# One-token attention and gated MLP over a 65,536-row cache: VectorE looped over heads 1 to 7, q projected in wide rows, the output projection in row form

## Chip, cores and metric

One NeuronCore of a Trainium2 chip. The metric is device time of one launch in microseconds (us). A profiled span is about 1.6 us shorter than the time of its launch (666.87 and 665.2 us before). A ratio is the mean time of one kernel's runs over the mean of the other's of the same rounds, so it is not quite the ratio of the medians that are quoted. A gain is clear of noise where the interval of the ratio leaves out 1. In the profiles PE is TensorE (matrix products) and PEld its weight loads, DVE is VectorE, ACT ScalarE, POOL GpSimd; SyncE issues the loads.

## The reference

```python
# bf16; x [1,1,512]; k_cache, v_cache [1,8,65536,128]; wq [512,4096]; wo [4096,512]
# w_gate, w_up [512,1792]; w_down [1792,512]
n = layernorm(x)
q = (n @ wq) as 32 heads of 128            # 4 query heads share one k/v head
s = q . k * 128**-0.5;  p = softmax(s);  o = p . v
h = x + o.reshape(1,1,4096) @ wo
m = layernorm(h)
out = h + (sigmoid(m @ w_gate) * (m @ w_up)) @ w_down
```

K and V are 268 MB of the 282 MB that are read. Every byte is used once for one token.

## The kernel before

SyncE issues loads into a ring of four 4 MB slots. A block is 4 MB, 16,384 rows of one head; K0 to K31 and V0 to V31 number the blocks over all eight heads. A K block is transposed by VectorE in eight pieces, TensorE makes scores of it; after four blocks comes the softmax; V blocks of the head before go through TensorE in between. Every load waits for its slot:

```python
order = [("wq", 0)]
order += [("K", b) for b in range(NR)]                   # NR = 4 blocks per head, NB = 32
for b in range(NR, NB):
    order += [("K", b), ("V", b - NR)]
order += [("V", NB-4), ("V", NB-3), ("V", NB-2), ("V", NB-1), ("wg", 0), ("wu", 0), ("wd", 0)]
# slot i % 4; a K slot is freed by VectorE's memset F{b} behind its eight transposes,
# a V slot by the last matmul PV{b} on it. wo is loaded into ktw (the transposed K) behind
# V(NB-4), and waits for the last score, S{NB-1}.
```

The program is a list of operations for each engine, written out one by one, except that TensorE's list of heads 1 to 7 is a loop (rounds must be equal, semaphores are counted down at the end of a round):

```python
def run(e, eng):                       # SyncE, GpSimd, ScalarE, VectorE: all written out
    seen = {}
    for o in self.ops[e]:
        put(e, eng, o, waits_of(o, seen, 0, False))
def run_pe(eng):                       # TensorE (head and tail cut)
    ...
    with eng.Fori(0, rounds):
        for o, w in zip(pe[c[0]:c[1]], plans[0]):
            put("pe", eng, o, w)
        for k, n in self.loop_sems.items():
            eng.sem_inc(..., -n)
```

The q projection and the output projection for 28 of the 32 heads:

```python
for kt in range(4):
    for n in range(NQ):                                  # 128 matmuls of 128 columns
        e.matmul(ps(1, 0, 128, 0, 32), lhsT=xz[:, kt*63 + 31-n : kt*63 + 63-n],
                 rhs=wq_v[:, kt, n*128:(n+1)*128], ...)
def project(rows, src, deps, last=False):                # 4 matmuls of one column for each row r
    for r in rows:
        for nt in range(4):
            e.matmul(ps(YT, nt, nt+1), lhsT=<wo row r, every 4th column from nt>, rhs=src[:, r:r+1], ...)
```

Compiled, VectorE's stream has 30,720 bytes, TensorE's 111,296, ScalarE's 9,280. The Trainium skill ("Perfetto Trace Analysis", The 4-stage abstract model) gives 64 bytes an instruction: 480, 1,739 and 145 instructions.

## Time and profile before

| | before |
|---|---|
| time, median of 4 runs | 666.88 us (666.58 to 667.7) |
| profiled span | 665.2 us |
| TensorE / VectorE / ScalarE busy | 63% / 53% / 6% |
| load queue, share of 16 engines' span | 99.0% |
| last V part: its first 3 MB reach TensorE | 646.46 us |
| up weights reach TensorE | 657.53 us |

From the page of the kernel before: span and busy rows. In part 2 each digit is the busy share of one fortieth of the span, in tenths; "DMA" is the mean of the sixteen DMA engines. Part 3 lists the DMA queues: q1 is the load queue, the two "instruction" queues are sequencers (an engine's instruction feeders) that fetch their own programs. A line has packets, MB, and the share of the sixteen engines' span.

```profile
span 665.2 us, 5117 instructions
PE 419.9 (63%) x2545; PEld 84.9 (13%) x1777; DVE 350.8 (53%) x441; ACT 39.7 (6%) x119; POOL 5.4 (1%) x12
...
DMA  9999999999999999999999999999999999999995
...
q1 hardware_dynamic: 11560, 282.33, 99.0%
q8 instruction: 6, 0.10, 0.1%
q14 instruction: 5, 0.04, 0.0%
```

The chain that ended last, as shares of the span:

```profile
DMA 72%; DVE 21%; PE 6%; issue 1%; SPq 0%; ACT 0%
```

The loads are the bound. VectorE's share of the chain is transposes that began because a K block had just landed. The interesting question is what, with DMA busy all the time, can still change. The landings at the end show where it is decided. Here is TensorE's timeline at the end (start, duration, what; in brackets its idle time just before, and what ended it):

```profile
629.43 3.61 PE L500 MATMUL PS<-ring,PT_sb 128*16 128x512 bf16 x32 [8.11 <-DMA ring<-in_A_v_cache_dram]
639.14 3.61 PE L500 MATMUL PS<-ring,PT_sb 128*16 128x512 bf16 x32 [6.10 <-DMA ring<-in_A_v_cache_dram]
646.46 3.61 PE L500 MATMUL PS<-ring,PT_sb 128*16 128x512 bf16 x32 [3.70 <-DMA ring<-in_A_v_cache_dram]
657.53 1.66 PE L581 MATMUL PS<-ring,hc 128*1 128x448 bf16 x16 [1.33 <-DMA ring<-in_B_w_up_dram]
```

These are V29, V30, the first 3 MB of V31, and the up weights. TensorE waits for each of them.

**How the lag of an engine is read.** A load is split over sixteen DMA engines, and each posts one completion increment. The Trainium skill ("DMA: Bandwidth & Descriptors", Why a DMA increments its semaphore by 16 and not by 1) says that only the full 16 means that all data has landed; in this trace too each load leaves 16 increments (4-byte packets on the load queue), and the reader starts behind the last. The last one's time minus the median of the sixteen is called *lag* below; *spread* is the last minus the first. No view of the profile shows it; a script computed it from the starts of these packets. The matmuls that wait begin about 0.5 us behind them (V30: last packet 638.63, matmul 639.14 us). The DMA packet records of the kernel before give:

| load | K1 | K8 | K16 | K24 | K31 | V30 |
|---|---|---|---|---|---|---|
| lag, us | 1.38 | 1.57 | 1.99 | 3.00 | 3.07 | 3.78 |

The median engine takes 9.71 us per load throughout. Single engines fall behind, in steps, and the steps coincide with packets of the instruction queues: 16 KB at 22, 77, 113, 615, 623 and 657 us, 8 KB at 56, 221, 224, 426 and 613 us. The 32 KB load packet behind an 8 KB fetch takes 1.59 or 1.88 us, where 1.22 us is the median. Behind a 16 KB fetch (TensorE's, 0.93 to 1.13 us) it takes 1.71 to 1.76 us. So one block of TensorE's costs about 1.5 us, one of VectorE's 1.0 us (0.33 for the fetch, 0.66 for the longer packet). At K24 four of the sixteen increments stand clearly apart from the rest, 1.32, 1.43, 1.62 and 3.00 us behind the median: this fits one TensorE block on each of three engines, and three VectorE blocks on a fourth. On this reading a TensorE block makes the worst lag up to K8, and VectorE's blocks from K16 on.

### The profile page before, as it was taken

To read this page: it belongs to the slowest core of one execution; us is meant where nothing else is said; L and a number is where in the kernel's file an instruction comes from. 1 tells how busy PE (TensorE), PEld (TensorE's weight loads), DVE (VectorE), ACT (ScalarE), POOL (GpSimd) and SP (SyncE) were. 2 spreads that over 40 slices of the span, in tenths; PEclk is the share of its full clock that TensorE was granted. 3 is DMA by queue.
4 is the path that set the end of the run, shared out by engine and by line. 5 is a ranking of instruction groups with operands and counts; after the bars stand their busy time and mean duration, and the time that the engine had idled before them with its cause. 6 is when DMAs were issued, how large, how long until landed. Compare 5 with 4: busy or idle time off the path is not lost.

```text
span 665.2 us, 5117 instructions
## 1 busy us (share of the span) xinstructions
PE 419.9 (63%) x2545; PEld 84.9 (13%) x1777; DVE 350.8 (53%) x441; ACT 39.7 (6%) x119; POOL 5.4 (1%) x12
## 2 busy tenths in 40 slices
PE   2787586557566675576765466766756667557445
PEld 2300011011000110011100110101100111002312
DVE  3598755566337655356555743367543655553002
ACT  0100200020000200020000200002000200002000
POOL 2000000000000000000000000000000000000000
PEclk9899598668887586877767788766778976766555
DMA  9999999999999999999999999999999999999995
GB/s 378 438 428 424 440 434 417 441 434 432 428 437 430 427 437 432 424 439 432 428 434 435 430 428 435 434 424 437 434 426 437 432 430 432 434 434 411 425 425 234
DMA packets 11573, 282.48 MB, mean 425 GB/s; under 512 B 1193, under 2 KB 2218, under 8 KB 2602
## 3 DMA queue, kind: packets, MB, share of 16 engines
q1 hardware_dynamic: 11560, 282.33, 99.0%
q8 instruction: 6, 0.10, 0.1%
q14 instruction: 5, 0.04, 0.0%
q10 hardware_dynamic: 2, 0.00, 0.0%
HBM read 282.33 MB, written 0.00 MB: 424 GB/s over the span
## 4 chain that ended last, share of the span: by engine, by line
DMA 72%; DVE 21%; PE 6%; issue 1%; SPq 0%; ACT 0%
DMA ring<-in_A_k_cache_dram 62%; DVE ktw L412 20%; DMA ring<-in_A_v_cache_dram 4%; DMA ring<-in_B_w_up_dram 4%; PE PS L424 3%; DMA ring<-in_A_wq_dram 2%; PE PS L370 1%; PE PS L423 1%; PE PS L500 1%; DVE PT_sb L468 0%; DVE M_sb L417 0%; PE PS L605 0%; PE PS L581 0%; SPq L300 0%; DVE hh L597 0%
## 5 line engine op out<-in xcount | busy, mean ns | idle before, releaser
L412 DVE STREAM_TRANSPOSE ktw<-ring 128x1024 f32<-128x1024 f32 x256 | 292.0, 1207 | 176.0 <-DMA ring<-in_A_k_cache_dram 175.6
L424 PE MATMUL PS<-ktw 128*128 128x512 bf16 x768 | 271.4, 452 | 55.2 <-DVE ktw L412 55.2
L423 PE MATMUL PS<-ktw 128*128 128x512 bf16 x256 | 118.7, 464 | 116.1 <-DVE ktw L412 116.1
L500 PE MATMUL PS<-ring,PT_sb 128*16 128x512 bf16 x1024 | 76.2, 449 | 18.0 <-DMA ring<-in_A_v_cache_dram 17.9
L423 PEld LDWEIGHTS PS<-ktw 128*128 128x128 bf16 x256 | 27.7, 108 | 432.9 <-issue 272.7
L500 PEld LDWEIGHTS PS<-ring,PT_sb 128*16 128x16 bf16 x1024 | 29.3, 116 | 63.3 <-issue 29.1
L468 DVE STREAM_TRANSPOSE PT_sb<-P_sb 128x512 bf16<-128x512 bf16 x32 | 20.2, 684 | 27.3 <-PE PS L500 25.7
L460 ACT ACTIVATE negmax<-PS 128x1 f32<-128x1 f32 x8 | 1.4, 171 | 548.8 <-PE PS L458 548.8
L417 DVE TENSOR_REDUCE M_sb<-PS 128x1 f32<-128x512 f32 x32 | 19.9, 682 | 25.4 <-PE PS L423 25.4
L465 ACT ACTIVATE P_sb<-PS,negmax 128x512 bf16<-128x512 f32 x32 | 21.6, 685 | 0.3
L514 DVE CAST O<-PS 128x4 bf16<-128x4 f32 x8 | 1.1, 138 | 34.7 <-PE PS L511 34.7
L479 DVE TENSOR_REDUCE lsum<-PS 128x1 f32<-128x4 f32 x8 | 1.3, 163 | 28.4 <-PE PS L477 28.4
L451 PE MATMUL PS<-identf,gm 128*1 128x128 f32 x16 | 3.2, 283 | 16.9 <-DVE gm L449 16.9
L370 PE MATMUL PS<-ring,xz 128*32 128x128 bf16 x128 | 9.1, 245 | 7.5 <-DMA ring<-in_A_wq_dram 7.5
L511 PE MATMUL PS<-sel_bf,po_sb 128*128 128x4 bf16 x32 | 2.1, 169 | 12.9 <-ACT po_sb L508 12.9
L370 PEld LDWEIGHTS PS<-ring,xz 128*32 128x32 bf16 x128 | 8.9, 112 | 7.5 <-issue 7.5
L390 ACT ACTIVATE ktw<-qc 32x16 bf16<-32x16 bf16 x32 | 8.5, 265 | 0.3
L508 ACT ACTIVATE po_sb<-PS,rl 128x512 bf16<-128x512 f32 x8 | 5.5, 687 | 41.0 <-PE PS L500 40.8
L458 PE MATMUL PS<-one_f,gmrep 1*128 1x1 f32 x16 | 4.2, 328 | 4.9 <-DVE gmrep L455 4.9
L465 ACT ACTIVATION_READ_ACCUMULATOR P_sb<-PS,negmax 128x1 f32 x32 | 6.5, 202 | 0.0
L345 POOL TENSOR_TENSOR rstd<-ve,nhalf 128x1 f32<-128x1 f32 x2 | 1.1, 555 | 648.7 <-DVE ve L343 648.7
L537 PE MATMUL PS<-O,ktw 128*128 128x1 bf16 x128 | 4.6, 172 | 0.3 <-DVE O L514 0.3
(78 smaller groups left out, 61.6 us busy)
## 6 DMA issues: line engine op xcount, KB each, us to landing
ring<-in_A_k_cache_dram SPq DMA_DIRECT2D x32, 4096.0 KB, 29.7
ring<-in_A_v_cache_dram SPq DMA_DIRECT2D x31, 4096.0 KB, 30.7
ring<-in_A_wq_dram SPq DMA_DIRECT2D x1, 4096.0 KB, 12.4
ring<-in_A_v_cache_dram SPq DMA_DIRECT2D x1, 3072.0 KB, 33.0
ktw<-in_A_wo_dram SPq DMA_DIRECT2D x1, 2048.0 KB, 11.4
ktw<-in_A_wo_dram SPq DMA_DIRECT2D x2, 1024.0 KB, 15.8
ring<-in_B_w_gate_dram SPq DMA_DIRECT2D x1, 1792.0 KB, 37.6
ring<-in_B_w_up_dram SPq DMA_DIRECT2D x1, 1792.0 KB, 24.4
```

The lines of the kernel that those rows point to most:

```text
L370: op("pe", lambda e, kt=kt, n=n, last=last: e.matmul(ps(1, 0, 128, 0, 32), lhsT=xz[:, kt * 63 + 31 - n: kt * 63 + 63 - n], rhs=wq_v[:, kt, ...
L390: op("act", lambda e, d=dst, s=src: e.activation(d, s, AF.Copy), ["qc", "Wz", f"S{NR * h - 1}" if h else None] if i == 0 else (), f"W{h}" ...
L412: op("dve", lambda e, d=dst, sr=src: e.transpose(d, sr), deps, f"T{b}.{c}", to="T")
L417: op("dve", lambda e, u=u: e.tensor_reduce(M_sb[:, u % 4:u % 4 + 1], ps(u % NS, 0, 512), AX.X, ALU.max), [f"S{b}.{NC - NR + k}"], f"mx{u}")
L423: return e.matmul(out, lhsT=lhsT, rhs=rhs, start=start, stop=stop)
L424: return e.add_instruction(mybir.InstMatmult(name=nc.get_next_instruction_name(), engine=mybir.EngineType.PE, ins=[e.lower_ap(rhs), e.lowe ...
L458: op("pe", lambda e: e.matmul(ps(MISC, 128, 129), lhsT=gmrep[0:1, :], rhs=one_f[0:1, 0:1], start=True, stop=True), [f"gmrep{h}"], f"neg{h}")
L465: op("act", lambda e, b=b: e.activation(P_sb[:, (b % 4) * 512:(b % 4 + 1) * 512], ps(b % NS, 0, 512), AF.Exp, bias=negmax[:, k:k + 1], sca ...
L468: op("dve", lambda e, b=b: e.transpose(PT_sb[:, (b % 4) * 512:(b % 4 + 1) * 512], P_sb[:, (b % 4) * 512:(b % 4 + 1) * 512]), [f"E{b}", f"P ...
L500: op("pe", lambda e, lhsT=lhsT, tq=tq, t0=t0, c=c: e.matmul(ps(PO, 0, 512, 32 * tq, 32 * tq + 16), lhsT=lhsT, rhs=ring[:, s * SLOT + t0 * ...
L508: op("act", lambda e: e.activation(po_sb[:, :], ps(PO, 0, 512), AF.Copy, scale=rl[:, k:k + 1]), [f"PV{NR * h + NR - 1}", f"rl{h}", f"ox{h ...
L537: op("pe", lambda e, lhsT=lhsT, r=r, nt=nt, end=end: e.matmul(ps(YT, nt, nt + 1), lhsT=lhsT, rhs=src[:, r:r + 1], start=False, stop=end, s ...
```

## The change

Its declared content: VectorE loops over heads 1 to 7, as TensorE does over all eight; q is projected eight heads wide; the attention output is projected in row form for 28 heads. To be loopable, every VectorE wait inside a round must be on a semaphore that VectorE alone counts down, so some dependencies move too.

```diff
-        def run_pe(eng): ...                 # the loop, for TensorE only
+        def run(e, eng):                     # the loop, for each engine in self.rounds
+            ...
+            with eng.Fori(lo, hi) as i:
+                for p in order:
+                    with ExitStack() as cond:
+                        if lo not in parts[e][p]:
+                            cond.enter_context(eng.If_ne(i.val[eng.engine], lo))
+                        for o, w in zip(parts[e][p][hi - 1], plan[p]):
+                            put(e, eng, o, w)
+                        ...                  # count this part's semaphores down
...
+        P.rounds = {"pe": (0, HKV), "dve": (1, HKV)}
...
-            for n in range(NQ):
+            for n in range(HKV):
...
-                    rhs=wq_v[:, kt, n * 128:(n + 1) * 128], start=(kt == 0 and n == 0), stop=last),
+                    rhs=wq_v[:, kt, n * 512:(n + 1) * 512], start=(kt == 0 and n == 0), stop=last),
...                                           # head_weights: 4 ScalarE copies a head become 1
-                        [f"S{NB - 1}"] if i == 0 else (), f"wo{i}")
+                        [f"G{HKV - 1}"] if i == 0 else (), f"wo{i}")      # G: memset behind the four maxima
...
-                   [f"E{b}", f"PV{NR * h - 1}" if h else None], f"PT{b}",
+                   [f"E{b}", f"oxq{h - 1}" if h else None], f"PT{b}", ...   # probability transposes
...
-            op("dve", lambda e: e.tensor_copy(O2[:, GS * h:GS * h + GS], ps(OX, 0, 4)), ...)
+            op("act", lambda e: e.activation(O2[:, GS * h:GS * h + GS], ps(OX, 0, 4), AF.Copy), ...)
...
+            for n, (r, src, deps) in enumerate(todo):      # 28 matmuls of 512 columns, a row of y
+                op("pe", lambda e, ...: e.matmul(
+                    ps(YB, 0, D, 0, 1), lhsT=src[:, r:r + 1], rhs=ktw[:, r * D:(r + 1) * D], ...))
+            op("dve", lambda e: e.tensor_copy(yr[:, :], ps(YB, 0, D, 0, 1)), ["yr"], "yrs")
+        def columns():                                      # later: the row back into 4 columns
```

## The prediction

> **What bounds it now.** The load queue. The page's DMA row is 9 tenths in 39 of 40 slices, its queue table gives the load queue 99.0% of the sixteen engines' span, and the timeline shows TensorE, VectorE and ScalarE waiting (busy 63%, 53%, 6%). The chain of waits is 72% DMA; its VectorE share (20%) is transposes that start when a K block lands, and each load is issued about 29.7 us before it lands, of which its own transfer is 9.71 us: some 20 us of slack per load. So nothing that only makes VectorE or TensorE busier or freer inside the stream can move the time.
>
> **What can.** A load lands when the slowest of its sixteen engines is done. In the trace's DMA packet records the sixteen completion increments of one load lie 0.6 us apart at the first load and 3.3 us at K31; at V30 4.3 us. The median engine never loses pace (9.71 us per load); single engines fall behind in steps of about 1.0 us, and each step falls on an instruction-fetch packet (queues "instruction" in the queue table: 16 KB for TensorE at 22, 77, 113, 615, 623 and 657 us; 8 KB at 56, 221, 224, 426 and 613 us), after which the next 32 KB packet takes 1.6 to 1.9 instead of 1.21 us. The Trainium skill ("Runtime: NRT & Kernel Launch", Instruction fetch mechanics) says a sequencer fetches its stream in blocks by its own DMA queue; this trace agrees (16 KB and 8 KB). 56, 224, 426 and 613 us are some 130 VectorE instructions apart, and their four steps make up the worst engine's lag. That lag is in the tail: the last V part lands at 648.93, up weights at 657.49, down at about 661 us; a median engine would be about 4 us earlier.
>
> **What the change does.**
> - VectorE's stream shrinks from 480 instructions to, by my count, about 200. It should fetch once or twice within the span instead of four times, if a jump back inside a resident block fetches nothing (TensorE's loop today fetches nothing from 113 to 615 us). Worst lag 4.3 -> about 1.9 us, the level of TensorE's own fetches: -2.0 to -2.4 us, on the critical path through the last loads.
> - q: 128 matmuls of 128 columns (9.07 us) become 32 of 512: about the same 7 to 10 us; ScalarE copies +2 us, head weights 1.11 -> 0.3 us. Off the path: K3 was issued at 22.3 and needed at 43 us.
> - Output projection: 3.9 us (112 matmuls) becomes 28 of 512 columns, 6 to 12 us in the gap before V29 lands at 629 us. Off the path.
> - wo is issued after the four maxima (2.5 us) instead of the last score: 601.8 -> about 602.3, since K31 lands 1.5 us earlier. Its first packet ran at 604.5, so no gap, at worst 0.5 us.
> - Probability transposes start 0.9 us later; branches in TensorE's loop cost tenths of a us: absorbed.
> - The tail after the last V part keeps its operations; one copy moves to ScalarE (0.16 -> 0.2 us).
>
> **Prediction.** 667.0 - 2.2 = about 664.8 us, range 663.0 to 667.4. Faster by over 2%: 0.005; within 2%: 0.98; slower: 0.015.
>
> **Shown right by:** fewer instruction packets in the queue table; no 8 KB fetches from 60 to 590 us; spread of increments at K31 below 2.3 us; last V part near 646.7, up weights near 655.3 us; VectorE busy unchanged at about 351 us.
>
> **Wrong if:** VectorE's loop fetches its block again each round (seven steps of 1 us on one engine: about 670 us); the later wo issue opens a gap; another engine's fetches already hold the tail at the same lag, so nothing is gained; or row projection runs past V29.

## The result, and the profile after

| | before | after |
|---|---|---|
| time, median of 4 runs each | 666.88 us | 664.5 us (664.23 to 664.6) |
| ratio | | 0.9962, 95% interval 0.9945 to 0.9979 |
| profiled span | 665.2 us | 662.6 us |
| instructions: VectorE, TensorE, ScalarE | 480, 1,739, 145 | 183, 1,268, 143 |
| median engine lands K31 | 585.32 us | 585.31 us |
| last engine lands K31 | 588.39 us | 586.91 us |
| last engine lands V30 | 638.63 us | 636.15 us |

The same lines of the page of the kernel after:

```profile
span 662.6 us, 4910 instructions
PE 424.0 (64%) x2385; PEld 80.5 (12%) x1617; DVE 350.6 (53%) x443; ACT 38.1 (6%) x106; POOL 5.4 (1%) x12
...
DMA  9999999999999999999999999999999999999997
...
q1 hardware_dynamic: 11560, 282.33, 99.3%
q8 instruction: 4, 0.07, 0.0%
q14 instruction: 2, 0.02, 0.0%
```

The chain that ended last, after:

```profile
DMA 71%; DVE 22%; PE 6%; issue 1%; SPq 0%; ACT 0%
```

And TensorE's timeline at the end, after:

```profile
626.94 3.21 PE L529 MATMUL PS<-ring,PT_sb 128*16 128x512 bf16 x32 [3.32 <-DMA ring<-in_A_v_cache_dram]
636.65 3.47 PE L529 MATMUL PS<-ring,PT_sb 128*16 128x512 bf16 x32 [6.50 <-DMA ring<-in_A_v_cache_dram]
643.98 3.22 PE L529 MATMUL PS<-ring,PT_sb 128*16 128x512 bf16 x32 [1.79 <-DMA ring<-in_A_v_cache_dram]
655.17 0.93 PE L632 MATMUL PS<-ring,hc 128*1 128x448 bf16 x16 [1.70 <-DMA ring<-in_B_w_up_dram]
```

VectorE is busy for the same 351 us, DMA moved the same bytes, and the pace of the loads did not move: the median engine lands K31 within 0.01 us of where it did. What moved is the last engine, by 1.48 us at K31 and by 2.48 us at V30, and the end follows it: 2.49 us at V29, 2.49 us at V30, 2.48 us at V31, 2.36 us at the up weights. Instruction packets fell from 6 to 4 (16 KB) and from 5 to 2 (8 KB). The faster up matmuls (0.93 for 1.66 us) fell in a stretch of higher granted clock in that execution (0.88 of full speed from 655 to 657.5 us); the control run of the same kernel below had 0.50 there, 1.66 us, and the same time.

### The profile page after: what moved, and what is told of

Its sections match the earlier page's. It is cut to its first block, busy times and chain, and to the rows that moved or that the text cites. A ratio compares the mean times of both kernels' runs of the same rounds, so it can differ in the third digit from the quotient of the medians.

```text
span 662.6 us, 4910 instructions
## 1 busy us (share of the span) xinstructions
PE 424.0 (64%) x2385; PEld 80.5 (12%) x1617; DVE 350.6 (53%) x443; ACT 38.1 (6%) x106; POOL 5.4 (1%) x12
## 4 chain that ended last, share of the span: by engine, by line
DMA 71%; DVE 22%; PE 6%; issue 1%; SPq 0%; ACT 0%
DMA ring<-in_A_k_cache_dram 62%; DVE ktw L439 20%; DMA ring<-in_A_v_cache_dram 4%; DMA ring<-in_B_w_down_dram 3%; PE PS L452 2%; DMA ring<-in_A_wq_dram 2%; PE PS L394 1%; PE PS L529 1%; DVE M_sb L444 1%; PE PS L451 1%; SPq L313 0%; DVE PT_sb L501 0%; PE PS L656 0%; PE PS L478 0%; PE PS L485 0%
## 5 line engine op out<-in xcount | busy, mean ns | idle before, releaser
L508 DVE TENSOR_REDUCE lsum<-PS 128x1 f32<-128x4 f32 x8 | 1.3, 162 | 29.8 <-PE PS L506 29.8
L394 PE MATMUL PS<-ring,xz 128*8 128x512 bf16 x32 | 9.7, 478 | 7.4 <-DMA ring<-in_A_wq_dram 7.4
L577 PE MATMUL PS<-ktw,O 128*1 128x512 bf16 x28 | 6.2, 379 | 0.0
L394 PEld LDWEIGHTS PS<-ring,xz 128*8 128x8 bf16 x32 | 3.2, 102 | 13.5 <-issue 11.3
L480 DVE TENSOR_REDUCE gmj<-PS 1x4 f32<-1x128 f32 x8 | 2.2, 278 | 4.1 <-PE PS L478 4.1
```

The lines of the kernel that those rows point to most:

```text
L394: op("pe", lambda e, kt=kt, n=n, last=last: e.matmul(ps(1, 0, 512, 0, 8), lhsT=xz[:, kt * 15 + 7 - n: kt * 15 + 15 - n], rhs=wq_v[:, kt, n ...
L577: op("pe", lambda e, r=r, src=src, n=n, end=end: e.matmul(ps(YB, 0, D, 0, 1), lhsT=src[:, r:r + 1], rhs=ktw[:, r * D:(r + 1) * D], start=( ...
```

## The experiments

**Theory.** The gain is VectorE's shorter stream. Each program block that a sequencer fetches during the loads sets one DMA engine back, for good, as long as no engine idles; the kernel ends by the engine that is furthest behind; VectorE's blocks fell on the one that was. **Rivals.** (a) The gain is in the two projections, or the shorter TensorE stream. (b) The gain is the VectorE loop as such, or fetches that stalled VectorE. (c) It is the moved issue of wo: an empty load queue around it. Where "worst engine" or "last engine" is used, the lag is read as above.

All edits are to the kernel after. E1 to E4 ran on one chip, E5 to E7 on one, E8 and E9 on one, each with the kernel before in the same rounds.

### E1: VectorE written out again

```diff
-        P.rounds = {"pe": (0, HKV), "dve": (1, HKV)}
+        P.rounds = {"pe": (0, HKV)}           # and VectorE's five counted-down semaphores removed
```

> The kernel after, with VectorE's stream written out again (490 instead of 183 instructions) and everything else kept. Theory (the gain is VectorE's three fewer instruction fetches, each a step of about 1 us on one DMA engine): VectorE fetches four 8 KB blocks within the loads again, the increments of K31 spread by 3.0 to 3.6 us instead of 1.94, and the time goes back to 666.3 to 667.2 us (ratio to the kernel before 0.999 to 1.0005). Rival (the gain is the shorter TensorE stream, the wide q, the row projection, or the moved wo issue): 664.5 us, ratio 0.996, as these are all still there.

Measured: 666.45 us (666.35 to 667.16), ratio 0.9994 (0.998 to 1.0007). VectorE fetched at 56, 223, 406 and 614 us; the spread of K31's increments was 3.20 us. The queue table, and TensorE's timeline for V31 and the up weights:

```profile
q8 instruction: 4, 0.07, 0.0%
q14 instruction: 5, 0.04, 0.0%
```

```profile
646.29 3.46 PE L529 MATMUL PS<-ring,PT_sb 128*16 128x512 bf16 x32 [1.64 <-DMA ring<-in_A_v_cache_dram]
657.38 0.93 PE L630 MATMUL PS<-ring,hc 128*1 128x448 bf16 x16 [1.57 <-DMA ring<-in_B_w_up_dram]
```

The two projections and TensorE's shorter stream are all here, and 0.4 us of the gain by the medians, not clear of nothing (the interval holds 1). Rival (a) falls.

### E2: the VectorE loop alone

The q projection, the head weights and the output projection of the kernel before, put back:

```diff
-            for n in range(HKV):              # 32 matmuls of 512 columns, and so on
+            for n in range(NQ):               # 128 matmuls of 128 columns, qc, 4 copies a head
...
-            todo = [...]; 28 row matmuls; yr; columns()
+            project(range(j0, j0 + nr), O3, ...)   # 112 matmuls of one column
```

> The kernel after, with q, the head weights and the output projection as before (TensorE's stream 1588 instead of 1268 instructions), so the VectorE loop is alone with what it needs. Theory: TensorE's one or two further fetches land on engines that are not the worst, K31's increments spread by less than 2.5 us, time 664.3 to 665.5 us (ratio 0.996 to 0.998). Rival (the gain is the two projections): 666.5 to 667 us, ratio 1.0.

Measured: 664.5 us (664.3 to 664.82), ratio 0.9962 (0.9949 to 0.9976): the whole gain. TensorE fetched six 16 KB blocks again, at 23, 47, 73, 621, 641 and 659 us, and the lag at K31 was 1.43 us, no more than after (1.60). At K8 four increments stand 0.81, 1.29, 1.42 and 1.44 us behind the median, after three TensorE blocks and one VectorE block: each seems to have fallen on an engine of its own.

### E3: 384 instructions for an idle engine

```diff
+        for i in range(384):
+            op("pool", lambda e, i=i: e.memset(pad[:, i:i + 1], 0.0))     # GpSimd, behind its last early task
```

> The kernel after, with 384 one-element memsets on GpSimd, an engine that has nothing to do between 7 and 650 us. They are done by about 40 us. Theory: GpSimd's sequencer fetches three further 8 KB blocks in the first 60 us, three steps of 1 us fall on one DMA engine and are never made up, K31's increments spread by 3.0 to 4.2 us, and the kernel is 1.2 to 2.2 us slower than the kernel after: 665.7 to 666.7 us (ratio 0.998 to 0.9995). Rival (the fetches cost time only by stalling VectorE, or the gain is in VectorE's own work): no change, 664.5 us, ratio 0.996.

Measured: 664.77 us (664.53 to 665.44), ratio 0.9967 (0.9953 to 0.998). **A miss**: slower than the kernel after by 0.3 us, not by 1.2 to 2.2. The three 8 KB fetches are there (14, 19 and 25 us), but each cost less than the 1.0 us that VectorE's cost: 0.31 us of its own, and the next load packet took 1.46 to 1.57 us, not 1.88. That is 0.55 to 0.67 us a block. The lag at K31 was 2.22 us, against 1.60. The time is nearer to the rival's number; the lag fits the theory with the smaller step. So small an effect decides nothing; E6 doubles it.

### E4: the loop kept, the length put back

```diff
+        for i in range(384):
+            op("dve", lambda e, i=i: e.memset(pad[:, i:i + 1], 0.0))      # VectorE, idle from 9 to 23 us
```

> The kernel after, with its VectorE loop, and 384 one-element memsets on VectorE in the head, in its idle time from 9 to 23 us: 567 instructions, four block borders instead of one. Theory: the loop is kept but four fetches are back, all in the first 60 us; K31's increments spread by about 4.3 us, time 666.4 to 667.2 us (ratio 0.9995), as before the change. Rival (the loop itself, not the length of the stream, is the gain): 664.5 us, ratio 0.996.

Measured: 666.66 us (666.36 to 666.86), ratio 0.9993 (0.9979 to 1.0006). VectorE fetched at 14, 19, 25 and 56 us, the lag at K31 was 4.13 us. VectorE had finished the memsets at 23.7 us and its first transpose, at 24.3 us, waited for K0 to land; 600 us later the kernel is still 2 us late:

```profile
646.46 3.61 PE L532 MATMUL PS<-ring,PT_sb 128*16 128x512 bf16 x32 [1.86 <-DMA ring<-in_A_v_cache_dram]
```

The loop as such gains nothing; rival (b) loses its first half.

### E5: control

> The kernel after, unchanged, as a control in the same rounds as the two below. Both theories: 664.3 to 664.8 us, ratio 0.996; K31's increments spread by 1.9 to 2.0 us.

Measured: the kernel after again, 664.48 us (664.3 to 665.04), ratio 0.9968 (0.9954 to 0.9981). Spread of K31's increments 2.11 us (slightly above the expected 2.0).

### E6: 768 instructions for an idle engine

As E3, with 768.

> As the kernel with 384 memsets on GpSimd, but 768: six further 8 KB blocks in the first 60 us. With 384 the three steps were 0.6 us each (the fetch 0.31 us, the next 32 KB packet 0.25 to 0.35 us longer), so six should come to about 3.6 us on GpSimd's DMA engine. Theory (the worst engine's lag is the time, whoever's instructions made it): K31's increments spread by 3.8 to 4.5 us and the time is 666.2 to 667.0 us, as the kernel before, though VectorE's loop and stream are those of the kernel after. Rival (only VectorE's own fetches cost, by stalling it): 664.5 to 664.8 us.

Measured: 666.64 us (666.61 to 666.71), ratio 0.9998 (0.9985 to 1.0012); lag at K31 3.87 us. All of the gain is gone, and VectorE's stream, loop and busy time are those of the kernel after. GpSimd's timeline shows the blocks themselves: the memsets come in groups of exactly 128 (128 x 64 bytes = 8 KB), with 0.5 us of idle time before the first of them and some 1.2 us before each of the others, for which the profile names no cause but issue. Each group starts 1.5 to 1.7 us after an 8 KB packet does (13.4, 18.7, 24.3, 29.8 and 35.3 us), so the wait is read as one for the next block:

```profile
14.89 4.27 POOL L392 MEMSET pad<- 1x1 f32 x128 [0.54 <-issue]
20.41 4.27 POOL L392 MEMSET pad<- 1x1 f32 x128 [1.25 <-issue]
25.94 4.27 POOL L392 MEMSET pad<- 1x1 f32 x128 [1.26 <-issue]
31.43 4.27 POOL L392 MEMSET pad<- 1x1 f32 x128 [1.23 <-issue]
36.95 2.59 POOL L392 MEMSET pad<- 1x1 f32 x77 [1.25 <-issue]
```

The queue table and the last landings of this run:

```profile
q8 instruction: 5, 0.08, 0.1%
q14 instruction: 8, 0.07, 0.0%
```

```profile
646.38 3.61 PE L532 MATMUL PS<-ring,PT_sb 128*16 128x512 bf16 x32 [1.65 <-DMA ring<-in_A_v_cache_dram]
657.43 1.66 PE L635 MATMUL PS<-ring,hc 128*1 128x448 bf16 x16 [1.98 <-DMA ring<-in_B_w_up_dram]
```

Instructions that no one waits for, done by 40 us, cost 2.2 us at 665 us (666.64 against 664.48 us of E5). Rival (b) falls.

### E7: 128 instructions for an idle engine

As E3, with 128.

> As above with 128 memsets: one further fetch on GpSimd's engine. Theory (only the worst of the sixteen engines counts): that engine reaches 0.3 to 1.1 us behind the median, less than the worst has anyway, so K31's spread stays 1.9 to 2.0 us and the time 664.3 to 664.8 us, equal to the control. Rival (each fetched block costs its share of time, wherever it lands: (2.3 us for 3 VectorE blocks, 0.8 us each): 665.2 us or more.

Measured: 664.19 us (663.93 to 664.36), ratio 0.9961 (0.9947 to 0.9975): nothing lost (0.1 us under the range, within noise), one more fetched block (at 13 us), lag at K31 1.56 us. A block that falls on an engine that is not the worst is free.

### E8: wo issued later

The slow variants raise a doubt. A late K31 makes the last score late, and with it the issue of wo: 604.2 us in E1, 604.5 in E4, 605.0 in E6, against 602.1 in the kernel after. In those three DMA idled for part of the stretch from 604 to 607 us. So a gap in the load queue, rival (c), might be what made them slow. E8 makes the gap without the lag:

```diff
-                        [f"G{HKV - 1}"] if i == 0 else (), f"wo{i}")
+                        [f"negmax{HKV - 1}"] if i == 0 else (), f"wo{i}")
```

> The kernel after, with the load of wo issued about 2 us later (it waits for the last head's negated maximum, not for the memset behind the four maxima): at about 604.2 us, where the slow variants (VectorE unrolled, padded VectorE, 768 memsets on GpSimd) issued it, at 604.2 to 605.0 us. In those, DMA was idle for part of the stretch from 604 to 607 us (share 0.55 to 0.69 against 0.88), so this gap is a rival cause of their time. Theory (the worst engine's lag is the time; it still has V28 to load until 606.3 us and does not idle): the gap shows in the DMA share (0.75 or less), the median engine lands V30 about 1 us later, the time stays at 664.3 to 664.9 us. Rival (the gap made the slow variants slow): 665.7 us or more.

Measured: 666.05 us (665.49 to 666.23), ratio 0.9985 (0.9971 to 0.9998). **A miss**: not unchanged, but 1.6 us slower than the control E5 by the medians. That ran on another chip; by the ratios to the kernel before (0.9985 and 0.9968) it is 1.1 us. The time lies in the range of the rival, so alone this run speaks for rival (c). Busy time by stretch, of the kernel after and of E8 (the last two columns are DMA share and GB/s):

```profile
604.00:607.00 3.00, 2.90 (x29) 1.24 (x32) 0.00 (x0) 2.86 (x9) 0.00 (x0) 0.50 0.88 371
```

```profile
604.00:607.00 3.00, 2.87 (x26) 1.33 (x30) 0.00 (x0) 2.58 (x8) 0.00 (x0) 0.50 0.64 158
```

The gap held the median engine back by 1.8 us (V30 at 636.44, after 634.62). I had compared that with the worst engine's lag of 1.6 us and forgotten that the others have blocks to take as well: the spread was down to 1.0 us behind the gap, and behind a TensorE block at 621 us one engine was 1.0 us behind the delayed median, and landed V30 last, at 637.41 us (after 636.15). So a gap has a price of its own, and it is paid through the last engine too. It can't be what the change gained, though: the kernels before and after have nearly the same DMA share in this stretch, 0.86 and 0.88. What is open is whether it made E1, E4 and E6 slow.

### E9: the lag without the gap

E6, with V29 issued ahead of wo, so that the queue holds a load when wo is late:

```diff
-            if ld == ("V", NB - 4):           # wo goes out behind this load
+            if ld == ("V", NB - 3):
```

> The kernel with 768 memsets on GpSimd, with V29 issued ahead of wo, so that the queue is not empty when wo is issued late: the gap is taken away and the lag is left. Theory: DMA share above 0.9 from 604 to 607 us, the worst engine at K31 still 3.8 to 4.0 us behind the median, time 666.2 to 667.0 us as with the gap. Rival (the gap is the cost): 664.3 to 665 us.

Measured: 666.7 us (666.33 to 666.89), ratio 0.9995 (0.9982 to 1.0009). DMA share from 604 to 607 us is 0.89 (above 0.9 was expected; the kernels before and after have 0.86 and 0.88), the lag at K31 is 3.74 us (3.8 to 4.0 expected), the median engine lands V30 at 634.79 us, on time, and the last at 638.62 us. Busy time by stretch of E6, then of E9, and E9's matmuls on V31:

```profile
604.00:607.00 3.00, 1.06 (x8) 0.71 (x12) 1.63 (x6) 0.16 (x1) 0.00 (x0) 0.83 0.55 158
```

```profile
604.00:607.00 3.00, 0.96 (x4) 0.58 (x4) 1.76 (x6) 0.03 (x1) 0.00 (x0) 0.84 0.89 382
```

```profile
646.46 3.61 PE L532 MATMUL PS<-ring,PT_sb 128*16 128x512 bf16 x32 [1.63 <-DMA ring<-in_A_v_cache_dram]
```

No gap, and the whole loss. (The new order alone, without the memsets, was not run; that it costs nothing itself is read from the median engine, which is on time.) Rival (c) can slow this kernel (E8), but is not the cause here.

### All runs by the last engine

| run | lag at K31 | V30, median engine | V30, last engine | time, median | time minus V30's last |
|---|---|---|---|---|---|
| before | 3.07 | 634.85 | 638.63 | 666.88 | 28.25 |
| after | 1.60 | 634.62 | 636.15 | 664.5 | 28.35 |
| E1 | 2.93 | 635.94 | 638.47 | 666.45 | 27.98 |
| E2 | 1.43 | 634.69 | 636.10 | 664.5 | 28.40 |
| E3 | 2.22 | 634.69 | 636.80 | 664.77 | 27.97 |
| E4 | 4.13 | 636.30 | 638.64 | 666.66 | 28.02 |
| E5 | 1.78 | 634.65 | 636.33 | 664.48 | 28.15 |
| E6 | 3.87 | 636.76 | 638.54 | 666.64 | 28.10 |
| E7 | 1.56 | 634.72 | 636.22 | 664.19 | 27.97 |
| E8 | 1.57 | 636.44 | 637.41 | 666.05 | 28.64 |
| E9 | 3.74 | 634.79 | 638.62 | 666.7 | 28.08 |

Landings are of the profiled execution, times are medians of all runs of the rounds, so some tenths are noise. The last column is constant to 0.7 us; the median engine's is no guide: before and E6 have it 1.9 us apart at the same time.

## Why the prediction was right

It said 664.8 us, -2.2 us; measured were 664.5 us, -2.4 us. Point by point:

- *The loads are the bound and have 20 us of slack each, so work inside the stream can't move the time.* Held. E1 has the wide q and the row projection, 160 matmuls fewer than the kernel before, and gains 0.4 us by the medians, which is not clear of noise; E2 has all those matmuls and the whole gain.
- *The lag of single DMA engines is the only lever, in steps at instruction fetches, and VectorE's four make the worst.* Held as far as tested (E8's gap is a second lever, for the worse), and shown from both sides: blocks taken away (after, E2), put back on VectorE (E1, E4), and put on an engine with no work (E6).
- *A jump back inside a resident block fetches nothing.* Held: VectorE fetched once, at 54.7 us, and then not at all in its seven rounds. The Trainium skill ("Runtime: NRT & Kernel Launch", Instruction fetch mechanics) warns that a taken branch to outside the resident blocks forces a fetch; no run here has a loop long enough to show that.
- *About 200 VectorE instructions.* 183.
- *Worst lag 4.3 to about 1.9 us* (there counted from the first increment to the last, at V30): 4.35 to 1.94. V31's last part was expected at 646.7 and TensorE's first weight load on it ran at 646.44 us; the up weights at 655.3, began at 655.17 us.
- *q takes 7 to 10 us, off the path.* 9.74 us, and K3's load was not late. (The one-copy head weights took 0.48 us, not 0.3, off the path too.) *Row projection 6 to 12 us in the gap before V29.* 6.2 us, done at 623.6, V29 at 626.9 us.
- *wo issued at about 602.3 us, no gap.* 602.09 us, DMA share as before. E8 shows how near this was: at 604.6 us it costs over 1 us. It stays early only because K31 now lands earlier.

That the number came out so close is not mere luck: the level of about 1.9 us agrees with the kernel before, where the second-worst engine lands K31 1.90 us behind the first, and did not rest on the size of a step. Two sentences of it were wrong in part. *No 8 KB fetches from 60 to 590 us*: there is one at 297.6 us. It is ScalarE's, which had been at 221 us: E2, which gives ScalarE its old copies back, has it at 222 us. It cost 0.7 us on an engine that was not the worst, so nothing. And *steps of about 1.0 us* is VectorE's size only: TensorE's 16 KB blocks cost about 1.5 us and GpSimd's 8 KB blocks 0.6 us. The second error lay in the expectation of E3; the first did no harm, as each TensorE block seems to fall on an engine of its own.

Open: why the packet behind VectorE's block is longer than behind GpSimd's, and which engine takes whose blocks. That all VectorE blocks fall on one engine is inferred from their steps adding up (E4: lag 2.81 us at K1 after three, 3.90 at V0 after four); the records don't name the DMA engine. Nor do they name whose an 8 KB packet is: that is read from which edit adds, removes or moves it. No version that clearly beats the kernel after was found: E2 and E7 equal it within noise. What is left, 1.6 us at K31, is TensorE's first two blocks (1.44 and 1.60 us), with VectorE's at 1.02 us close behind; none of the edits here would remove them all.

## What to carry to other kernels

This is the evidence of one kernel. When a kernel keeps all DMA engines busy from its first to its last load, look at the slowest of them, not at the mean: here a few microseconds put on a single engine early were still there at the end. Program length was then a cost, even on engines that have time to spare, so loop a long stream or shorten it, and judge that by where its blocks fall: a block on an engine that isn't the worst is free. Before trusting a load issued just in time, work out how many tenths of a microsecond lie between its issue and an empty queue, for the median engine as well as for the last.

## What the Trainium skill lacked or had wrong

- "Runtime: NRT & Kernel Launch", Instruction fetch mechanics: says refills come in 16 KB blocks. TensorE's do; VectorE's, ScalarE's and GpSimd's come in 8 KB (128 instructions; GpSimd's memsets run in groups of 128).
- The same section: says that crossing a block border is mostly hidden. It is not where loads saturate DMA: each block set one DMA engine back, by 0.6 us (GpSimd), 1.0 us (VectorE) or about 1.5 us (TensorE's 16 KB), until the load queue next ran empty; three fewer VectorE blocks gave 2.4 us of 667, while a block on an engine that was not the worst cost nothing (E7). GpSimd itself also stood idle some 1.2 us before each block in E6.
- The same section: gives the fetch stall at a branch out of the resident blocks as a reason to prefer full unrolling. It does not say what follows where the target is resident: VectorE's loop here fetched nothing in its seven rounds, and is the faster form (ratios to the kernel before: 0.9962 with the loop, 0.9994 without it in E1), by its shorter stream and not as a loop (E4).
- "DMA: Bandwidth & Descriptors", Specifications: gives about 27 GiB/s per engine. A 32,768-byte packet took 1.218 us (median of 8,192): 26.9 GB/s in powers of ten, where 27 GiB/s would be 1.13 us.
- No page has it: with the load queue full, a load's landing drifts behind the median by single engines (0.6 us spread at the first load, 3.3 us at K31 before the change), and keeps that lag until the queue runs empty (E8: spread 1.0 us behind the gap, at the price of 1.8 us for the median).
